# Infini-attention with a gated feed-forward on one core: memory reads and their scaling moved into the gate/up phases, value projections moved between the first transposes, phi in two VectorE steps

## Chip, core and metric

The kernel runs on one core of one Trainium2 chip. The metric is device time of one execution in microseconds (us). Before the change the median of 14 runs is 299.04 us (296.95 to 301.62).

## What is computed

The input x has 2048 rows of 448 columns in bfloat16, H = 16 heads of Dh = 28 columns, and the rows are cut into 4 segments of L = 512. The reference, cut to what matters:

```python
xn = layernorm(x)
q, k, v = xn @ wq, xn @ wk, xn @ wv          # (B, H, segment, L, Dh)
phi = lambda t: where(t > 0, t + 1.0, exp(t))
g = sigmoid(beta)
M = 0; z = 0
for s in range(4):
    p = softmax(q[s] @ k[s].T * Dh ** -0.5 + causal_mask)
    a_dot = p @ v[s]
    a_mem = (phi(q[s]) @ M) / (phi(q[s]) @ z + 1e-6)
    out[s] = g * a_mem + (1 - g) * a_dot
    M += phi(k[s]).T @ v[s]; z += phi(k[s]).sum(rows)
S = concat(out) @ wo
G = silu((gelu(xn @ w_gate) * (xn @ w_up)) @ w_down)   # w_gate, w_up: 448 x 1792
return x + S * G
```

## The kernel before

The order of the work is written out by hand (`tc.manual_schedule()`): every engine runs its instructions in the order in which the program issues them, and TensorE, VectorE, ScalarE and GpSimd each wait at their own head of queue. All DMAs on SP likewise stand in one queue. So "later in the program" means "behind" on every engine that an operation uses.

**Tiles.** A segment has NB = 4 blocks of 128 rows; D = 448 is padded to NDC = 4 chunks of 128; heads go in G = 4 groups of HG = 4, each head padded to 32 columns. Queries and keys are kept transposed (head columns on partitions, 512 rows along the free axis), values with rows on partitions and a column of ones beside each head (`vaug`), so that a product with V also gives the softmax's sum. PSUM has three pools: `ps_s` (two tiles of 128 x 1024, for scores and for gate/up), `ps_pv` (one), `ps_m` (three tiles named `m`, for all else).

**Stages** (times of the profiled execution):

- Head, 0 to 29.3 us: 100 idle matmuls on zeros (line 93), loads, layer norm of segment 0 (`layer_norm`, lines 226 to 263), per block a scaling on VectorE (`scale_x`, line 250), four TensorE transposes and a ScalarE copy (`turn`, lines 260 and 261), then `project_units(0)`: eight q/k units (line 302) and four v units (line 335, evicted on VectorE at line 337). One pair of tiles `xns` holds the scaled blocks in turn.
- Gate/up 0, 29.3 to 57.4 us: `gate_up` (line 466 on) has 14 steps `fc`. Each has four matmuls with w_gate and four with w_up into one `s` tile (line 474), a gelu on ScalarE (`gl`, line 477), a product on VectorE (`hT`, line 478), and whatever a table of steps holds for step `fc`. At full clock a step is 1.73 us of TensorE. In steps of gate/up 0 stand the layer norm of segment 1 (transposed by DMA, line 256) and `guard`, a check of the weights' size whose squares go into tiles named `pqT` and `xr`.
- Attention 0, 57.4 to 90; gate/up 1, 90 to 113.8; attention 1, 113.8 to 157.9; gate/up 2 and 3, 157.9 to 207; attention 2, 207 to 234; attention 3, 234 to 268.
- Tail, 268 us to the end: the rest of segment 3's down projections (`d3[2:]`, 18 units), its last combinations and the output.

**Attention** (`attention`). There are 12 score steps k (4 groups x 3 banks). Step k issues scores on TensorE (line 378), exp on ScalarE (line 384), a causal mask on GpSimd (line 388), and the product with V of step k-2 (line 399, `give`). Each step has two half steps; in each, a table `at` may add work, and filler units (projections of the next segment, down projections, output products) are issued while the TensorE work done is less than `due`, which the planner computes: `own` and `ours` are its costs of scores and products in us, `tot` the cost of all filler, `theirs` the running ScalarE cost (1.3, 1.3 or 0.88 per half step; 27.84 at the end).

```python
theirs.append((theirs or [0.0])[-1] + (1.3, 1.3, 0.88)[bk])
...
due = (own + tot) * theirs[n - 1] / theirs[-1] - ours[n - 1]
```

The last two products of a segment are returned as `ends` and issued in the stage after.

**phi** (lines 312 to 328) follows a projection by two ticks of a clock: exp on ScalarE (line 315); then, a tick later, three VectorE steps: u = t + 1 (line 319), e = min(e, 1) (line 321), max(u, e) (line 323). phi(k) goes into a tile `pkT` of a pool with two buffers, and SP transposes it by DMA into `pkb` (line 325). phi(q) goes into `pqT`.

**Dividing.** `evac` (line 407 on) copies an accumulated product to SBUF (VectorE, line 412) and sends the rows with the sums by SP to a compact tile `dc` (line 416). `invert` (line 425 on) scales and inverts `dc` on VectorE (lines 430 and 432), splits it on GpSimd into three bf16 `terms` (lines 435 and 437) and sends them by SP into `rows` (line 438). `inverses` (line 446) spreads `rows` over the partitions by a matmul into an `m` tile. `combine` (lines 458, 462, 463) scales the attention part with it and adds the memory part; `scale_memory` (line 451) scales the memory part; `memory_read` (line 422) multiplies phi(q) with the memory and calls `evac`.

**Where these stand before.** The memory reads of segments 1 and 3 are the first filler of attentions 1 and 3 (`pre`), their inversion and scaling stand in the table `at`. Those of segment 2 stand in gate/up 3. The last two products, the inversion and the combinations of segment s are issued by `tail`, in the next gate/up phase (segment 2: in attention 3; segment 3: in the tail).

## Time and profile before

| What | Value |
|---|---|
| Median of 14 runs | 299.04 us (296.95 to 301.62) |
| The profiled execution's own time | 300.53 us |
| Its span, first to last instruction | 298.7 us |
| Mean granted TensorE clock | 0.956 |
| Mean of one gelu (line 477), ScalarE | 597 ns |
| Mean of one exp, 1024 and 512 columns (line 384) | 1021 ns and 598 ns |
| Mean of one table load, ScalarE | 1283 ns |
| Mean of one copy of 512 columns out of PSUM, VectorE (line 412) | 681 to 686 ns |
| phi's three steps, VectorE (lines 319, 321, 323) | about 300, 530, 450 ns |

The profile is of one execution. PE is TensorE's matmul, PEld its weight loads, DVE VectorE, ACT ScalarE, POOL GpSimd, SP the engine that issues most DMAs; a q behind the name is the engine's sequencer. "L474" is line 474 of the kernel. "out<-in" names the tiles. In brackets or after the bar stands the idle time of the engine just before, and the instruction that ended it. The row PEclk gives in 40 slices the clock that TensorE was granted, in tenths of full speed. Matmuls overlap, so a busy share near 1 for TensorE does not say that the array works at its peak.

### The profile page before, as it was taken

The page shows a single profiled execution, that of the slowest core. Times are in us where ns is not written, and L with a number is a line of the kernel's source. Part 1 is how long each engine was busy: PE and PEld are TensorE (multiplying, and loading weights), DVE is VectorE, ACT ScalarE, POOL GpSimd, SP SyncE. Part 2 cuts the span into 40 slices and gives each one's busy share as a digit, 9 for nine tenths or more (in the row PEclk, how much of TensorE's full clock was granted, in tenths as well). Part 3 has the DMA queues.
Part 4 walks back from the last instruction along what each step waited for, and adds up shares of the span by engine and source line. Part 5 has one row for each costly group of instructions (what it writes and reads, how often), then busy time and mean ns, then how long its engine had stood idle before and what let it go on. Part 6 is the DMA issues. An engine that isn't in the chain of part 4 may idle for free. (4 is left out here: it accounts for less than half of the span.)

```text
span 298.7 us, 4626 instructions
## 1 busy us (share of the span) xinstructions
PE 264.2 (88%) x1652; PEld 116.6 (39%) x1652; DVE 189.3 (63%) x381; ACT 151.3 (51%) x215; POOL 98.0 (33%) x217
## 2 busy tenths in 40 slices
PE   7695999989999997989999999999799879893960
PEld 7442344434444443333344444544233323341420
DVE  6655376346687767478787666557566634862863
ACT  3352264569894333786673333334979566760010
POOL 4100010044440300765450233120667455485000
PEclk9887799999999999999999999999899968999798
DMA  8998002300100053001110120001000000001002
GB/s 242 357 329 111 18 2 50 82 2 1 38 19 19 9 98 101 3 24 34 35 35 19 26 53 2 4 8 61 15 19 16 24 7 10 3 32 36 3 5 69
DMA packets 26354, 15.11 MB, mean 51 GB/s; under 512 B 17872, under 2 KB 25044, under 8 KB 26324
## 3 DMA queue, kind: packets, MB, share of 16 engines
q1 hardware_dynamic: 23392, 10.20, 14.7%
q10 hardware_dynamic: 2324, 3.16, 3.2%
q0 software_dynamic: 608, 1.38, 1.3%
q8 instruction: 15, 0.25, 0.3%
q14 instruction: 15, 0.12, 0.1%
HBM read 9.18 MB, written 1.84 MB: 37 GB/s over the span
## 5 line engine op out<-in xcount | busy, mean ns | idle before, releaser
L384 ACT ACTIVATE pt<-s 128x1024 bf16<-128x1024 f32 (+1 forms) x96 | 79.1, 880 | 24.5 <-PE s L378 22.8
L388 POOL TENSOR_SCALAR_AFFINE_SELECT pt<-pt 128x256 bf16<-128x256 bf16 x128 | 50.5, 417 | 86.7 <-ACT pt L384 85.0
L477 ACT ACTIVATE gl<-s 128x512 bf16<-128x512 f32 x56 | 33.4, 597 | 70.6 <-PE s L474 51.7
L478 DVE TENSOR_TENSOR hT<-gl,s 128x512 bf16<-128x512 bf16 x56 | 38.4, 686 | 36.4 <-ACT gl L477 35.6
L474 PE MATMUL s<-xnT,wg_sb 128*128 128x512 bf16 x224 | 58.9, 386 | 0.2 <-DVE hT L478 0.2
L474 PE MATMUL s<-xnT,wu_sb 128*128 128x512 bf16 x224 | 58.4, 384 | 0.0
L489 PE MATMUL m<-wd_sb,hT 128*128 128x448 bf16 x224 | 52.9, 369 | 0.9 <-DVE oU L462 0.9
L474 PEld LDWEIGHTS <-wu_sb 128*128 128x128 bf16 x224 | 22.1, 99 | 27.1 <-issue 1.1
L474 PEld LDWEIGHTS <-wg_sb 128*128 128x128 bf16 x224 | 21.9, 100 | 27.3 <-issue 3.1
L489 PEld LDWEIGHTS <-hT 128*128 128x128 bf16 x224 | 21.4, 101 | 24.8 <-issue 7.3
L378 PE MATMUL s<-qT,kT 32*128 32x512 bf16 (+3 forms) x256 | 21.8, 312 | 5.8 <-ACT pt L384 5.6
L246 POOL TENSOR_TENSOR rstd<-rstd,nhalf 128x2 f32<-128x2 f32 x8 | 5.7, 707 | 57.1 <-DVE rstd L244 57.1
L302 PE MATMUL m<-xnT,wq_pad 128*128 128x512 bf16 x64 | 17.8, 395 | 2.2 <-ACT xnT L261 0.9
L492 ACT ACTIVATE th<-m 128x448 f32<-128x448 f32 x16 | 8.6, 546 | 21.4 <-PE m L489 16.3
L335 PE MATMUL m<-wv_sb,xnT 128*128 128x448 bf16 x64 | 15.9, 381 | 3.8 <-DVE vaug L337 3.5
L399 PE MATMUL pv<-pt,vaug 128*32 128x512 bf16 (+3 forms) x256 | 18.2, 317 | 1.0 <-POOL pt L388 0.6
L378 PEld LDWEIGHTS <-kT 32*128 32x128 bf16 x256 | 6.8, 92 | 27.2 <-issue 26.9
L302 PE MATMUL m<-xnT,wk_pad 128*128 128x512 bf16 x64 | 17.4, 391 | 0.0
L306 DVE CAST kT<-m 128x512 bf16<-128x512 f32 x16 | 11.0, 686 | 9.6 <-PE m L302 9.5
L412 DVE COPY oU<-pv 128x512 f32<-128x512 f32 x16 | 11.0, 686 | 9.5 <-PE pv L399 9.4
L446 PE MATMUL m<-rows,spread 128*128 128x512 bf16 x28 | 11.1, 402 | 6.4 <-DMA rows<-terms 6.1
L518 PE MATMUL m<-wo_sb,oT 128*128 128x448 bf16 x64 | 15.2, 360 | 0.9 <-DVE oT L463 0.9
(100 smaller groups left out, 282.5 us busy)
## 6 DMA issues: line engine op xcount, KB each, us to landing
x_sb<-in_A_x_dram SPq DMA_DIRECT2D x7, 224.0 KB
wd_sb<-in_B_w_down_dram SPq DMA_DIRECT2D x1, 1568.0 KB
wg_sb<-in_B_w_gate_dram SPq DMA_DIRECT2D x1, 1344.0 KB
wu_sb<-in_B_w_up_dram ACTq DMA_DIRECT2D x1, 1344.0 KB
out_dram<-o_out POOLq DMA_DIRECT2D x12, 112.0 KB, 2.0
xr<-in_A_x_dram ACTq DMA_DIRECT2D x2, 448.0 KB
out_dram<-o_out SPq DMA_DIRECT2D x4, 112.0 KB
wo_sb<-in_A_wo_dram SPq DMA_DIRECT2D x4, 98.0 KB
```

The costliest lines, as they stand in the source:

```text
L302: nc.tensor.matmul(out=pr[:], lhsT=wpad[nm][:, c, g * HG:(g + 1) * HG, :].rearrange("p h d -> p (h d)"), rhs=xnT[s][:, c, :], start=(c == ...
L335: nc.tensor.matmul(out=vp[:, 0:D], lhsT=xnT[s][:, c, b * P:(b + 1) * P], rhs=wv_sb[:, c, :], start=(c == 0), stop=(c == NDC - 1))
L378: nc.tensor.matmul(out=sp[i // 2][:, i % 2, c0:c0 + n], lhsT=kT[s][r, g, kb * P:(kb + 1) * P], rhs=qT[s][r, g, kb * P:L], start=True, stop ...
L384: nc.scalar.activation(out=pt[:, :, 0:w], in_=sp[pr][:, :, 0:w], func=ACT.Exp, scale=scale)
L388: nc.gpsimd.affine_select(out=v, in_=v, pattern=[[0, 2], [1, P]], compare_op=ALU.is_ge, fill=0.0, base=0, channel_multiplier=-1)
L399: nc.tensor.matmul(out=acc[i * HP:(i + 1) * HP, kb * P:L], lhsT=va[:, kb, g * HG + i, :], rhs=pts[i // 2][:, i % 2, c0:c0 + n], start=(kb ...
L446: nc.tensor.matmul(out=r[:], lhsT=spread[:, g, :], rhs=rows[side][:], start=True, stop=True)
L474: nc.tensor.matmul(out=gu[:, i, :], lhsT=w_sb[:, c, fc * P:(fc + 1) * P], rhs=xnT[s][:, c, :], start=(c == 0), stop=(c == NDC - 1))
L477: nc.scalar.activation(out=gl[:], in_=gu[:, 0, :], func=ACT.Gelu_apprx_tanh)
L478: nc.vector.tensor_tensor(out=hT[s][:, fc, :], in0=gl[:], in1=gu[:, 1, :], op=ALU.mult)
L489: nc.tensor.matmul(out=d_ps[:, 0:D], lhsT=hT[s][:, fc, b * P:(b + 1) * P], rhs=wd_sb[:, fc, :], start=(fc == 0), stop=(fc == NFC - 1))
L518: nc.tensor.matmul(out=a_ps[:, 0:D], lhsT=oT[s][:, g, b * P:(b + 1) * P], rhs=wo_sb[:, g, :], start=(g == 0), stop=(g == G - 1))
```

## The change

The diff touches six things.

1. The head issues 145 idle matmuls, and issues the v unit of block b-1 after block b's transposes; the last v unit follows the padding of wk. The eight q/k units come after.
2. phi takes two VectorE steps: e = min(e, 1), then one `scalar_tensor_tensor` that computes max(t + 1, e). The pool of `pkT` has three buffers; for segment 0, phi(k) has a tile of four slots, which takes the buffer named `pqT`.
3. `theirs` in attention begins from 2.6 instead of 0.
4. `evac` can copy on ScalarE. It does for the last product of segments 0 and 1 and for the memory reads of segments 1 and 2, all in gate/up phases.
5. Memory reads, inversion and scaling of segment 1 go from attention 1 into gate/up 1 (steps 0 to 3, 6, 10 to 13), where the inversion of segment 0's sums goes from step 5 to 4 and its combinations from steps 10 on to 7 on. In gate/up 3 the inversion goes from step 6 to 4, the scaling from 10 to 8. The reads of segment 3 go from the start of attention 3 to half steps 5 to 8, their inversion to 13, their scaling to 17 to 20; there segment 2's inversion goes from half step 5 to 4 and its combinations from 10 to 9.
6. In the tail the first inversion splits its terms on VectorE, and the three combinations begin one unit later, so that the last group's inversion stands ahead of the third of them.

```diff
-        pkp = pool("pkp", 2)
+        pkp = pool("pkp", 3)
...
-        for i in range(100):
+        for i in range(145):
...
+            units0.extend(project_units(0))
+            v = units0[8:]
             for b in range(NB):
                 scale_x(b)
                 turn(b)
+                if b:
+                    run(v[b - 1:b])
             pad_weight("wk")
+            run(v[NB - 1:])
...
+            if s == 0:
+
+                pk0 = seg1.tile([P, G, L], BF16, name="pqT")
+
             def phi(g, nm, dst):
                 e = work.tile([P, L], BF16, name="ph_e")
-                u = seg1.tile([P, L], BF16, name="ph_u")
                 nc.scalar.activation(out=e[:], in_=dst[:, g, :], func=ACT.Exp)
-                ph = pqT[s][:, g, :] if nm == "wq" else pkp.tile([P, L], BF16, name="pkT")[:]
+                if nm == "wq":
+                    ph = pqT[s][:, g, :]
+                else:
+                    ph = pk0[:, g, :] if s == 0 else pkp.tile([P, L], BF16, name="pkT")[:]
 
                 def rest():
-                    nc.vector.tensor_scalar(out=u[:], in0=dst[:, g, :], scalar1=1.0, scalar2=None,
-                                            op0=ALU.add)
                     nc.vector.tensor_scalar(out=e[:], in0=e[:], scalar1=1.0, scalar2=None,
                                             op0=ALU.min)
-                    nc.vector.tensor_tensor(out=ph, in0=u[:], in1=e[:], op=ALU.max)
+                    nc.vector.scalar_tensor_tensor(out=ph, in0=dst[:, g, :], scalar=1.0, in1=e[:],
+                                                   op0=ALU.add, op1=ALU.max)
...
-            nc.vector.tensor_copy(out=t, in_=ps[:])
+            (copy or nc.vector.tensor_copy)(out=t, in_=ps[:])
...
-                    theirs.append((theirs or [0.0])[-1] + (1.3, 1.3, 0.88)[bk])
+                    theirs.append((theirs or [2.6])[-1] + (1.3, 1.3, 0.88)[bk])
...
+        units0 = []
         layer_norm_first()
-        run(project_units(0))
+        run(units0[:8])
...
-        table = tail(0, {}, ends, 5, 10)
+        table = tail(0, {}, ends, 4, 7, nc.scalar.copy)
+        memory(1, table, 0, 6, 10, nc.scalar.copy)
...
-        pre = [(0.22, [lambda g=g: memory_read(1, g)]) for g in range(G)]
-        at = memory(1, {}, 99, 5, 10, 2)
-        ends = attention(1, pre + merge([(0.9, [lambda: update(1)])], pu[8:12])
-                         + merge(down_units(1), finish_units(0), pu[:8]), at)
+        ends = attention(1, merge([(0.9, [lambda: update(1)])], pu[8:12])
+                         + merge(down_units(1), finish_units(0), pu[:8]))
...
-        table = tail(1, {}, ends, 5, 10)
+        table = tail(1, {}, ends, 5, 10, nc.scalar.copy)
...
-        table = memory(2, {}, 0, 6, 10)
+        table = memory(2, {}, 0, 4, 8, nc.scalar.copy)
...
-        at = tail(2, {}, ends, 5, 10)
-        pre = [(0.22, [lambda g=g: memory_read(3, g)]) for g in range(G)]
-        memory(3, at, 99, 6, 14, 2)
-        ends = attention(3, pre + d2[2:] + merge(finish_units(2), d3[:2]), at)
+        at = memory(3, tail(2, {}, ends, 4, 9), 5, 13, 17)
+        ends = attention(3, d2[2:] + merge(finish_units(2), d3[:2]), at)
...
-        table = {0: [lambda: invert(3, 0, 0, G - 1)], 1: ends[:1], 3: ends[1:],
+        table = {0: [lambda: invert(3, 0, 0, G - 1, nc.vector)], 1: ends[:1], 3: ends[1:],
                  8: [lambda: invert(3, 0, G - 1, G, **fast)]}
-        in_turn(table, 5, [lambda g=g: combine(3, g) for g in range(G - 1)])
+        in_turn(table, 6, [lambda g=g: combine(3, g) for g in range(G - 1)])
```

## The prediction

> **What bounds the kernel now.** I read busy shares first, then busy time by stage, then TensorE's waits, then the timeline around each long wait. The page:

> ```profile
> PE 264.2 (88%) x1652; PEld 116.6 (39%) x1652; DVE 189.3 (63%) x381; ACT 151.3 (51%) x215; POOL 98.0 (33%) x217
> ...
> PEclk9887799999999999999999999999899968999798
> ```

> TensorE is the bound on average, but its clock row dips in four regions: the first 35 us, and around 215, 245 and 278 us. Cutting the span at the stage borders shows where it is not full (time, PE busy, PEld, DVE, ACT, POOL, clock):

> ```profile
> 0.00:29.30 29.30, 21.61 (x165) 14.01 (x165) 17.27 (x56) 11.07 (x16) 4.99 (x13) 0.90 0.96 265
> ...
> 157.90:207.00 49.10, 49.07 (x240) 22.75 (x240) 31.57 (x58) 15.75 (x27) 11.06 (x18) 1.00 0.07 15
> 207.00:234.00 27.00, 24.39 (x185) 9.00 (x184) 18.23 (x33) 23.01 (x29) 17.55 (x38) 0.94 0.11 35
> 234.00:268.00 34.00, 30.01 (x219) 11.35 (x217) 19.13 (x33) 21.65 (x28) 18.48 (x48) 0.90 0.05 13
> 268.00:298.70 30.70, 15.53 (x78) 6.65 (x76) 16.50 (x30) 2.06 (x4) 5.78 (x12) 0.91 0.09 28
> ```

> Gate/up of segments 2 and 3 (157.9 to 207) is solid TensorE; nothing off TensorE can be gained there. Head, attention 2, attention 3 and tail have holes. TensorE's waits, in total, times, longest:

> ```profile
> PE m L446 <- DMA rows<-terms: 6.1, 2, 4.5
> PE s L378 <- ACT pt L384: 5.6, 9, 1.2
> PE m L335 <- DVE vaug L337: 3.5, 2, 3.4
> ...
> PE m L422 <- DVE oT L458: 1.4, 1, 1.4
> ```

> The clock by 3.4 us stretches gives the second half of the price. Stretches with PE busy 1.10 (23.4:26.8), 1.41 (9.8:13.2), 1.90 (211.2:214.6), 1.75 (238.5:241.9) and 0 us (272.6:276) were each followed by half clock; stretches at 2.28 (112.2:115.6), 2.31 (269.2:272.6) and 2.43 us (231.7:235.1) were not. So holes cost twice.

> ```profile
> 211.20:214.60 3.40, 1.90 (x22) 0.70 (x21) 1.86 (x3) 2.81 (x5) 3.09 (x7) 1.00 0.09 34
> 214.60:218.00 3.40, 3.40 (x26) 0.98 (x18) 1.72 (x5) 2.55 (x4) 1.38 (x4) 0.50 0.02 5
> ```

> [...]

> **The change, part by part.** Times are of the profiled execution (300.53 us, span 298.7).

> *Head.* Now the third phi result waits 3.48 us for one of two pkT buffers, held by a DMA transpose; the v evictions queue behind it on VectorE, TensorE waits 3.35 us, and the clock is halved until 33.7. Gate/up 0 starts at 29.30 with 4.4 us of half clock ahead, worth 2.2 us: as if at 31.5. In the new order segment 0's phi(k) gets four slots (no wait), and v runs among the transposes. The 45 extra idle matmuls at some 0.055 us (the rate of the last 55 of the 100: 3.0 us) end near 11.9, so block 0's transposes slip from 11.22 by 0.7 us. Then a serial chain: copy of block 0 (589 ns), v 0 (4 matmuls, 0.75), its eviction 0.62, and only behind it on VectorE the scaling of block 2 (0.38); transposes 0.25, v 1, and so on, about 2.2 us per block with handoffs. v 3 ends near 19.1, then eight q/k units of 0.86: gate/up starts near 26. The order of ScalarE shows a cost that the diff hides: the fourth phi(k) now falls behind the first gelu, so exp and gelu tables are loaded again: 2 x 1.283 + 0.63 = 3.2 us between the first two gelus. Gelu 1 ends 6.2 us after the stage starts, the VectorE product at 6.9, while TensorE wants that buffer for its fourth step at 5.2: 1.7 us of stall. Behind these loads on ScalarE wait all later gelus; the check's squares must also wait for the phi buffer, which carries the same name, about 0.3 us and covered. Effective start 27.7 against 31.5: 3.8 us gained with a full clock. The chain keeps TensorE busy about 2.0 us per 3.4, between 1.90 (halved) and 2.28 (kept), so I cannot decide it; half clock costs 1.5 to 3. I take 2.5, range 0.5 to 4.

> *phi in two steps.* Three rows, 310 + 530 + 442 ns, become 530 + x; x lies between 442 (as the two-tensor row) and about 690 (612 scaled by 512/448). I take 690: 0.06 us x 24 = 1.5 us of VectorE; at 442, 7 us. The cover is TensorE; nothing is counted apart.

> *Earlier fill in attention (the 2.6).* Filler matmuls are due sooner, by 2.6/30.44 = 8.5% of a stage's TensorE work at its start, none at its end. Attention 0: scores wait 0.63 us for exp at 63.3 and v 0.34 us earlier; 0.7 taken (0 to 1). Attention 2: waits 1.07 and 0.63 us plus the half clock of 214.6:218, which costs about 1.5; but ScalarE has 24.9 us of work there (16 x 1.021 + 8 x 0.598 = 21.1, four phi exps 2.5, a table load 1.3) in 27.0, so at most 2.1 to 2.5. Taken 1.5 (0 to 2.5).

> *Memory reads of segment 1.* At 114 to 117 us four reads wait for VectorE: excesses of 1.5, 0.4 and 0.4 us, 2.3 in all. They go into gate/up 1, evicted by ScalarE (about 0.6 us each; it has 1.13 us idle per step there). Matmuls, 8 x 0.22 with the scalings, move and do not vanish. VectorE in attention 1 loses 4 x 0.68 + 4 x 0.68 = 5.4 us, and TensorE waits 0.57, 0.50, 0.28 and 0.23 us behind VectorE in it; some of that goes, and with the earlier fill the 0.58 us at 121.3. Taken 2.8 (1.5 to 4). In gate/up 1 the first inversion now has three steps (5.2 us) until its rows are read; in the trace of before this takes 4.65 us from VectorE's step (100.65) to landing (third DMA issued at 103.25 plus 2.0, as in the tail). VectorE at up to 2.05 us in one step of 1.73 is covered by two score buffers. The new dc and rows DMAs pass SP ahead of the x transposes, delaying block 1's by about 2 us; the last still lands before attention 1. Taken -0.2 (-1 to 0). Gate/up 3: the inversion comes two steps earlier and VectorE waits about 0.4 us for dc, covered.

> *Attention 3.* Four reads leave its start: 0.78 + 0.57 + 0.22 us wait, while ScalarE idles 3.58. Then scores wait 1.19 and 0.63, and two half-clock stretches (241.9 to 248.7) of 5.9 us of matmul time lose 3.0. At 254 one more 0.95 us wait, for PSUM. Sum 7.3; what is late next is ScalarE, 24 exps and four tanh in 34. The reads come back at half steps 5 to 8, evicted by VectorE. I take half: 3.5 (1 to 6).

> *Tail.* The longest wait:

> ```profile
> 271.87 0.56 POOL L530 DMA_DIRECT2D out_dram<-o_out  x1 [0.30 <-POOL o_out L529]
> 272.43 0.25 POOL L435 CAST terms<-dc 96x64 bf16<-96x64 f32 x1
> 272.70 2.66 SPq L438 DMA_DIRECT2D rows<-terms  x3
> ...
> 275.46 0.59 SPq L416 DMA_DIRECT2D dc<-oU  x1
> ...
> 276.63 0.59 PE L446 MATMUL m<-rows,spread 128*128 128x512 bf16 x1 [4.47 <-DMA rows<-terms]
> ```

> The reciprocal was ready at 269.6; GpSimd, behind masks and outputs, took it up at 272.43. On VectorE the five small operations (0.19 to 0.22) end at 270.8, three issues on SP of 0.8 end near 272.5, rows landed near 273.5: 3.1 us earlier. The combine moves one unit (0.58 us) later, so 4.5 us of wait become about 0.8; with that hole the half clock of 276:279.4 (about 1.4) likely goes. The last group's dc DMA, behind these on SP, issues near 272.5 instead of 275.46, and its inversion now stands ahead of the third combine (1.37 us). Left at the end, about 1 us instead of 1.68. Sum 5.7; the output chain after it (12 us) is unchanged. I take 4.2 (1.5 to 5.7).

> **Sum.** 2.5 + 0.7 + 1.5 + 2.8 - 0.2 + 3.5 + 4.2 = 15.0: 285.5 from the profiled 300.53. That execution is 1.5 above the median of 299.04; some of the 1.5 may be clock loss already in the sum. I put 285.

> **Rivals.**
> *The clock is not granted.* Holes shrink but stay thin, head and both late attentions stay half clocked, or ScalarE binds: head 1.0, attention 0 0.7, gate/up 1 -0.2, attention 1 2.8, attention 2 0.3, attention 3 1.5, tail 3.5: 9.6, so 291. For: the head's 2.0 lies in the undecided gap. Against: the tail's wait is a plain queue on GpSimd.
> *Everything goes.* Upper ends, about 22: 278. For: the terms are separate waits. Against: ScalarE's 24.9 us in attention 2.
> *Slower: fill starves ScalarE.* In-order TensorE puts 8.5% of a stage's 28 to 40 us (2.4, 3, 1.8, 1.8 = 9.0 us) ahead of the scores; if ScalarE is then the bound to each stage's end, it is lost in full and replaces the 8.5 us that attentions gain: 300.5 - 2.5 + 0.2 - 4.2 + 9.0 = 303. It decides once more than about 6.5 of the 9.0 us is lost. For: ScalarE waits 22.8 us for scores in all. Against: in attentions 0 and 1 it has slack (30.18 of 44.1 busy in attention 1).

> **How the numbers follow.** About 0.3% is what a measurement can tell from no change. Forecast (281 to 288) 0.58; clock not granted (288 to 296) 0.23; everything 0.14; slower 0.04; no change 0.01. The range 279.5 to 291.5 leaves out the far ends.

> **What would show it.** Right: no wait of TensorE on v's eviction, full clock after about 20 us, two more table loads of 1283 ns after the first gelu with one stall of 1 to 2 us, reads without waits in gate/up 1, terms on VectorE in the tail with its row wait under 1.5 us. Wrong: half clock from 16 to 24 us, a row wait in gate/up 1 over 1 us, attention 3 still near 34 us, or phi's second step well over 0.7 us.

## The result and the profile after

The changed kernel takes 294.92 us (median of 10 runs, 293.91 to 297.93), the kernel before 299.28 (median of 47 runs): a ratio of 0.989 with a 95% interval of 0.986 to 0.992. The ratios count the fast runs of a kernel alone, those within 1.5% of the fastest beside them, and by that rule the profiled executions of the kernel before and of experiment 7 are slow ones. The changed kernel is faster, by 4.4 us instead of the 14 that I forecast, and lies outside my range. Its profiled execution took 294.19 us with a span of 292.2, against 300.53 and 298.7 before, so 6.5 us of the span are to be explained. About 2 of them come from the choice of the two executions, since one lies 0.7 us below its kernel's median and the other 1.3 above. Differences below between two variants are of medians; where they are small the ratios to the kernel before decide, since each was taken with runs of that kernel on the same chip.

The page of the kernel after, busy time by engine and TensorE's granted clock in 40 slices:

```profile
PE 260.1 (89%) x1697; PEld 116.9 (40%) x1697; DVE 185.1 (63%) x352; ACT 157.7 (54%) x227; POOL 100.3 (34%) x212
...
PEclk9999999999999999999999999999999999796698
```

The dips of the first 35 us and of 215 us are gone. What is left sits in the last fifth, and there it is deeper than before. The same by stage (time, busy of PE, PEld, DVE, ACT, POOL, clock, then DMA share and GB/s): head, gate/up 0 with attention 0, gate/up 1 with attention 1, gate/up 2 and 3, attention 2, attention 3, tail.

```profile
0.00:25.90 25.90, 21.80 (x209) 15.76 (x210) 16.07 (x48) 8.86 (x14) 4.99 (x13) 1.00 0.94 286
25.90:84.40 58.50, 56.25 (x357) 24.21 (x356) 36.86 (x72) 42.01 (x60) 16.84 (x36) 1.00 0.16 33
84.40:145.10 60.70, 60.27 (x391) 26.24 (x389) 44.70 (x81) 38.89 (x57) 24.85 (x52) 1.00 0.18 42
145.10:199.20 54.10, 53.91 (x271) 24.57 (x269) 32.85 (x60) 21.64 (x37) 12.38 (x21) 1.00 0.08 17
199.20:225.80 26.60, 24.62 (x189) 9.26 (x188) 17.32 (x28) 22.82 (x29) 18.49 (x40) 1.00 0.12 37
225.80:258.60 32.80, 27.45 (x211) 10.31 (x210) 19.55 (x34) 21.33 (x28) 19.40 (x46) 0.95 0.05 13
258.60:292.20 33.60, 15.81 (x77) 6.53 (x76) 17.70 (x34) 2.17 (x4) 3.32 (x6) 0.81 0.08 25
```

Five stages run at a full clock; only the last two do not. Reading where stages start in the two timelines (the first gate/up matmul, the first and the last score) gives the balance in us. (These borders replace the stage times given ahead of the forecast, which lie up to 4.5 us later: gate/up 2 starts at 153.4, not at 157.9.)

| stretch | before | after | change | my step |
|---|---|---|---|---|
| head and gate/up 0 | 0 to 59.0 | 0 to 55.4 | -3.6 | -2.5 |
| attention 0 | 59.0 to 88.1 | 55.4 to 84.4 | -0.1 | -0.7 |
| gate/up 1 and attention 1 | 88.1 to 153.4 | 84.4 to 145.1 | -4.6 | -2.6 |
| gate/up 2 and 3 | 153.4 to 207.6 | 145.1 to 199.2 | -0.1 | 0 |
| attention 2 and 3, to the last score | 207.6 to 265.7 | 199.2 to 256.2 | -1.1 | -5.0 |
| tail, from the last score | 265.7 to 298.7 | 256.2 to 292.2 | **+3.0** | -4.2 |

The row of attention 2 and 3 hangs on the execution. Experiment 3 below runs the program of the kernel before, changed in the tail alone, and in its profiled execution every other stretch ahead of the tail agrees with this table within 0.2 us. Attention 2 and 3, however, take 55.4 us there (207.8 to 263.2) instead of 58.1. The two, from 27.7 us after the first score of attention 2 on, first the kernel before, then experiment 3:

```profile
235.30:265.70 30.40, 26.98 (x201) 9.98 (x199) 17.43 (x30) 20.56 (x26) 15.53 (x39) 0.89 0.05 10
235.50:263.20 27.70, 24.32 (x200) 9.75 (x200) 17.54 (x30) 20.45 (x26) 15.45 (x39) 1.00 0.05 11
```

The same instructions run once with a stretch of half clock and once without it, 2.7 us apart. Against experiment 3 the changed kernel's 57.0 us are 1.6 us slower, not 1.1 faster.

At 199 us the kernel is 8.4 us ahead, more than the 5.8 that my steps give to that point. The tail gives 3.0 back where I had 4.2 to gain. TensorE's waits (total, times, longest) name the cause:

```profile
PE m L456 <- DMA rows<-terms: 10.8, 4, 5.9
PE s L388 <- ACT pt L394: 3.4, 10, 0.6
PE s L484 <- DVE hT L488: 2.2, 3, 1.8
```

The v evictions are no longer among the long waits (3.5 us before), and the scores wait 3.4 us instead of 5.6. But the spread matmuls wait 10.8 us for inverse rows, where it was 6.1. The longest of these waits, in the timeline of the tail: VectorE's first cast of the terms, two row waits of TensorE, and the DMA issues of SP and GpSimd.

```profile
259.12 1.68 DVE L445 CAST terms<-dc 96x64 bf16<-96x64 f32 x1
260.86 2.66 SPq L448 DMA_DIRECT2D rows<-terms  x3
264.78 0.38 PE L456 MATMUL m<-rows,spread 128*128 128x512 bf16 x1 [2.60 <-DMA rows<-terms]
...
269.68 0.68 SPq L448 DMA_DIRECT2D rows<-terms  x1
...
271.31 0.64 POOL L448 DMA_DIRECT2D rows<-terms  x1 [9.72 <-issue]
273.12 0.61 PE L456 MATMUL m<-rows,spread 128*128 128x512 bf16 x1 [5.91 <-DMA rows<-terms]
```

Three groups' rows were sent from 260.86 and the first combines used them at 264.78 and 265.37. The third combine needs no other row. Yet its spread matmul at 273.12 waits 5.91 us, until just behind the row DMAs of 269.68 to 271.31, which carry the rows of the last group, for which it has no use. In the code the reason is in two lines: `combine(3, 2)` now falls on unit 8, behind the last group's inversion of the same unit, and the spread matmul takes all of `rows[side]` as its operand (L456), into which that inversion writes (L448 to L449). The clock is half from 265.85 to 276.09, three windows of 3.41 us. The first stands behind the wait of 2.60 us and begins before the hole of 5.91 us; the hole keeps the clock down for two more. (From 262.44 on TensorE is busy 0.97, 1.28, 0 and 2.97 us of each 3.41; the last three of these are at half clock.)

In attention 3 the same pair of operations waits again. The timeline, then a cut in stretches of 3.4 us:

```profile
244.95 1.92 SPq L448 DMA_DIRECT2D rows<-terms  x3
248.25 0.38 PE L456 MATMUL m<-rows,spread 128*128 128x512 bf16 x1 [2.04 <-DMA rows<-terms]
```

```profile
236.00:239.40 3.40, 2.50 (x16) 0.84 (x17) 3.08 (x5) 3.17 (x5) 2.27 (x5) 1.00 0.11 21
239.40:242.80 3.40, 3.02 (x25) 1.14 (x25) 3.33 (x6) 1.78 (x3) 0.95 (x3) 1.00 0.00 1
...
246.20:249.60 3.40, 1.36 (x12) 0.43 (x8) 1.20 (x2) 0.77 (x2) 3.09 (x7) 0.88 0.11 17
249.60:253.00 3.40, 3.15 (x18) 0.87 (x15) 1.25 (x2) 1.94 (x2) 1.58 (x4) 0.62 0.10 34
```

The memory inversion of segment 3 starts at half step 13 (243.64 on VectorE), and its rows arrive after the scaling wants them; TensorE then has 1.36 us of work in 3.4 and loses the clock. VectorE is full from 236 to 242.8 (3.08 and 3.33 us), which made me suspect the four reads that now stand there.

### The profile page after: what moved, and what is told of

The parts are those of the page before. It is cut to its first block, busy times and chain, and to the rows that moved or that the text cites. A ratio compares the mean times of both kernels' runs of the same rounds, so it can differ in the third digit from the quotient of the medians.

```text
span 292.2 us, 4695 instructions
## 1 busy us (share of the span) xinstructions
PE 260.1 (89%) x1697; PEld 116.9 (40%) x1697; DVE 185.1 (63%) x352; ACT 157.7 (54%) x227; POOL 100.3 (34%) x212
## 3 DMA queue, kind: packets, MB, share of 16 engines
q0 software_dynamic: 608, 1.38, 1.3%
## 5 line engine op out<-in xcount | busy, mean ns | idle before, releaser
L398 POOL TENSOR_SCALAR_AFFINE_SELECT pt<-pt 128x256 bf16<-128x256 bf16 x128 | 53.8, 444 | 80.4 <-ACT pt L394 79.4
L484 PE MATMUL s<-xnT,wg_sb 128*128 128x512 bf16 x224 | 57.5, 379 | 2.2 <-DVE hT L488 2.2
L484 PE MATMUL s<-xnT,wu_sb 128*128 128x512 bf16 x224 | 57.5, 379 | 0.0
L499 PE MATMUL m<-wd_sb,hT 128*128 128x448 bf16 x224 | 52.0, 364 | 0.2 <-DVE oU L472 0.2
L499 PEld LDWEIGHTS <-hT 128*128 128x128 bf16 x224 | 20.8, 100 | 23.3 <-issue 6.4
L456 PE MATMUL m<-rows,spread 128*128 128x512 bf16 x28 | 11.1, 401 | 12.1 <-DMA rows<-terms 10.8
L409 PE MATMUL pv<-pt,vaug 128*32 128x512 bf16 (+3 forms) x256 | 17.5, 311 | 0.0
L307 PE MATMUL m<-xnT,wq_pad 128*128 128x512 bf16 x64 | 17.0, 380 | 0.0
L422 DVE COPY oU<-pv 128x512 f32<-128x512 f32 x14 | 9.6, 683 | 10.4 <-PE pv L409 10.4
L311 DVE CAST qT<-m 128x512 bf16<-128x512 f32 x12 | 8.3, 690 | 11.1 <-PE m L307 11.0
L345 PE MATMUL m<-wv_sb,xnT 128*128 128x448 bf16 x64 | 14.7, 353 | 0.6 <-ACT xnT L261 0.5
```

The costliest lines, as they stand in the source:

```text
L307: nc.tensor.matmul(out=pr[:], lhsT=wpad[nm][:, c, g * HG:(g + 1) * HG, :].rearrange("p h d -> p (h d)"), rhs=xnT[s][:, c, :], start=(c == ...
L345: nc.tensor.matmul(out=vp[:, 0:D], lhsT=xnT[s][:, c, b * P:(b + 1) * P], rhs=wv_sb[:, c, :], start=(c == 0), stop=(c == NDC - 1))
L398: nc.gpsimd.affine_select(out=v, in_=v, pattern=[[0, 2], [1, P]], compare_op=ALU.is_ge, fill=0.0, base=0, channel_multiplier=-1)
L409: nc.tensor.matmul(out=acc[i * HP:(i + 1) * HP, kb * P:L], lhsT=va[:, kb, g * HG + i, :], rhs=pts[i // 2][:, i % 2, c0:c0 + n], start=(kb ...
L456: nc.tensor.matmul(out=r[:], lhsT=spread[:, g, :], rhs=rows[side][:], start=True, stop=True)
L484: nc.tensor.matmul(out=gu[:, i, :], lhsT=w_sb[:, c, fc * P:(fc + 1) * P], rhs=xnT[s][:, c, :], start=(c == 0), stop=(c == NDC - 1))
```

## The experiments

My theory after the result: the mechanisms in head, attention 1 and attention 2 were right; two edges of the new order cost what the rest of the change gains, the false dependency in the tail and the late inversion in attention 3. Rivals: the late inversion's place on VectorE and SP costs, whichever tile it writes; the reads crowd VectorE; the earlier fill does harm.

**1. The last group's inversion one unit later**, behind the third combine.

```diff
-                 8: [lambda: invert(3, 0, G - 1, G, **fast)]}
+                 9: [lambda: invert(3, 0, G - 1, G, **fast)]}
```

> The changed kernel with the last group's inversion in the tail issued after the third combination (unit 9, not 8); TensorE's order is the same. Theory: the third combination's spread matmul reads the whole rows tile, so in the changed kernel it waits for the last group's rows DMAs, which the program issues just ahead of it; that is the 5.91 us wait at 273.1 us and the reason for half clock until 276. Then the wait falls under 0.5 us, and although the inversion itself comes 1.4 us later on VectorE the time falls by about 5 us, to about 290. Rival: the last group's rows set the end anyway (its inversion is on the path, and it is now later): no gain, or up to 1 us slower, 295 to 296.

Measured: 288.09 us (287.78 to 291.15), ratio 0.964 (0.960 to 0.969). One digit gives 6.8 us. Third and last spread matmul of its tail:

```profile
267.44 0.58 PE L456 MATMUL m<-rows,spread 128*128 128x512 bf16 x1 [0.27 <-DVE oU L472]
274.62 0.39 PE L456 MATMUL m<-rows,spread 128*128 128x512 bf16 x1 [0.93 <-DMA rows<-terms]
```

The 5.91 us are gone from the third; the last group's own wait is 0.93 us. Behind the first row wait (2.63 us here) one window is at half clock, 266.38 to 269.79, instead of three, and another from 276.62 (the 13 output matmuls from 276.52 take 4.32 us, 2.63 in experiment 2). So the place matters. It doesn't yet tell the tile from the queues.

**2. A row buffer of its own for the last group**, with the order left as it is after the change: its inverses are written into `rows[1]` and read from there.

```diff
-                    out=rows[side][32 * i + g0 * HG:32 * i + g1 * HG, :].rearrange(
+                    out=rows[side if to is None else to][32 * i + g0 * HG:32 * i + g1 * HG, :].rearrange(
...
-            o_a, r, dst = oU.pop((s, g, 0)), inverses(0, g), oT[s][:, g, :]
+            o_a, r, dst = oU.pop((s, g, 0)), inverses(int(s == NSEG - 1 and g == G - 1), g), oT[s][:, g, :]
...
-        fast = dict(eng=nc.vector, queues=[nc.sync, nc.scalar, nc.gpsimd])
+        fast = dict(to=1, eng=nc.vector, queues=[nc.sync, nc.scalar, nc.gpsimd])
```

> The kernel after with its order unchanged; only the last group's inverses are written into and read from the other row buffer, so that the combine of the third group no longer depends on the last group's row transfers. Theory (the dependency on a shared tile is what costs): the 5.91 us wait goes and the time falls as in the run with unit 9, to 288 to 290. Rival (the queue places of the late inversion cost, on VectorE and SP, whichever tile it writes): no change, 294 to 296.

Measured: 287.32 us (286.92 to 289.52), ratio 0.959 (0.954 to 0.963). Its third and last spread matmul:

```profile
269.89 0.38 PE L456 MATMUL m<-rows,spread 128*128 128x512 bf16 x1 [0.59 <-DVE oU L472]
275.75 0.39 PE L456 MATMUL m<-rows,spread 128*128 128x512 bf16 x1 [0.76 <-DMA rows<-terms]
```

The inversion still stands ahead of the third combine on VectorE and SP, and the wait is gone all the same. It was the shared tile, not the queues. From the last score (259.0) to the end of the span (287.7) it takes 28.7 us, 4.3 less than before: the tail's gain that I had forecast (4.2). The same tail in the second combination of experiment 10 takes 29.6 us (252.1 to 281.7), with one window of half clock at 261.45 that this execution lacks: the third spread matmul takes 0.59 us there and 0.38 here.

**3. The terms of the tail on VectorE alone, in the kernel before.**

```diff
-        table = {0: [lambda: invert(3, 0, 0, G - 1)], 1: ends[:1], 3: ends[1:],
+        table = {0: [lambda: invert(3, 0, 0, G - 1, nc.vector)], 1: ends[:1], 3: ends[1:],
```

> The kernel before with one edit: the terms of the first inversion of the tail are computed on VectorE instead of GpSimd; the combines stay at units 5 to 7, ahead of the last group's inversion at unit 8. Theory (my tail step was right about the terms and failed only on the order of the third combine): the first row wait falls from 4.47 us to about 2.5 and part of the half clock behind it goes, 1.5 to 4 us less than before, 295.5 to 298. Rival (the terms were never what the rows waited for, SP's queue was): no change, 298.5 to 300.

Measured: 297.54 us (296.53 to 299.05), ratio 0.993 (0.990 to 0.996). Its VectorE and SP at the start of the tail, and its first row wait:

```profile
267.90 1.29 DVE L435 CAST terms<-dc 96x64 bf16<-96x64 f32 x1
269.22 0.22 DVE L437 TENSOR_TENSOR dc<-dc,terms 96x64 f32<-96x64 f32 x1
```

```profile
272.16 0.57 PE L446 MATMUL m<-rows,spread 128*128 128x512 bf16 x1 [2.44 <-DMA rows<-terms]
```

The wait of 4.47 us falls to 2.44, not to 0.8. The part alone gains 2.2 us (0.7% of 299.9; 1.3 to 3.0 by the interval). The two traces don't place it: of their 3.3 us of span 0.8 lies in the tail (32.2 us from the last score instead of 33.0), and 2.7 in attention 3, where the programs are the same.

**4. The memory inversion of segment 3 at half step 11 instead of 13.**

```diff
-        at = memory(3, tail(2, {}, ends, 4, 9), 5, 13, 17)
+        at = memory(3, tail(2, {}, ends, 4, 9), 5, 11, 17)
```

> The changed kernel with the inversion of segment 3's memory sums in attention 3 at half step 11 instead of 13 (its rows are read from half step 17). Theory: attention 3 lost its gain to a new wait, the rows landing 2.0 us too late for the first scaling at 248.3 us, and the half clock that this hole brings (248.8 to 252.2): 2 to 3.5 us faster, 291.5 to 293. Rival: attention 3 is bound by ScalarE, and the wait only takes up slack: within 0.5 us of 294.9.

Measured: 293.23 us (292.72 to 293.56), ratio 0.980 (0.977 to 0.983). Its row wait, and the stretch behind it:

```profile
247.05 0.38 PE L456 MATMUL m<-rows,spread 128*128 128x512 bf16 x1 [0.81 <-DMA rows<-terms]
```

```profile
248.80:252.20 3.40, 2.60 (x22) 0.96 (x21) 2.06 (x4) 1.86 (x3) 2.56 (x6) 1.00 0.10 34
```

2.04 us of wait became 0.81, and the half clock of attention 3 went. By medians this is 1.7 us, a little under the theory's range. Attention 2 and 3 take 54.8 us from the first score of attention 2 (199.1) to the last of attention 3 (253.9), against 57.0 after the change.

**5. Attention 3 arranged as before**: reads first as filler, output units from 5 and 10, inversion at 6, scalings at 14, 16, 18, 20.

```diff
-        at = memory(3, tail(2, {}, ends, 4, 9), 5, 13, 17)
-        ends = attention(3, d2[2:] + merge(finish_units(2), d3[:2]), at)
+        at = tail(2, {}, ends, 5, 10)
+        pre = [(0.22, [lambda g=g: memory_read(3, g)]) for g in range(G)]
+        for i, f in enumerate([lambda: invert(3, 1)]):
+            at.setdefault(6, []).append(f)
+        for i in range(G):
+            at.setdefault(14 + 2 * i, []).append(lambda g=i: scale_memory(3, g))
+        ends = attention(3, pre + d2[2:] + merge(finish_units(2), d3[:2]), at)
```

> Attention 3 alone is arranged as in the kernel before: the four memory reads of segment 3 as filler at its start, output units from half steps 5 and 10, memory inversion at 6, scalings at 14, 16, 18, 20; all else as in the kernel after (294.9 us). Theory: the rearrangement of attention 3 cost about as much as it gave, since the reads at half steps 5 to 8 fall on a VectorE that is full (3.08 and 3.33 of 3.40 us) and the late inversion makes TensorE wait 2.04 us for rows: 293.5 to 296.0. Rival (my prediction's step, 3.5 us gained by moving the reads): undoing it costs 2 us or more, 297 to 299.

Measured: 291.83 us (291.25 to 292.5), ratio 0.974 (0.970 to 0.979). Better than my theory had it, and far from the rival's 297 to 299: undoing this part gains about 3 us. Attention 2 and 3 take 54.5 us (198.5 to 253.0), at a full clock.

**6. The reads alone put back**, with the inversion at 11.

```diff
-        at = memory(3, tail(2, {}, ends, 4, 9), 5, 13, 17)
-        ends = attention(3, d2[2:] + merge(finish_units(2), d3[:2]), at)
+        at = tail(2, {}, ends, 4, 9)
+        in_turn(at, 11, [lambda: invert(3, 1)])
+        in_turn(at, 17, [lambda g=g: scale_memory(3, g) for g in range(G)])
+        pre = [(0.22, [lambda g=g: memory_read(3, g)]) for g in range(G)]
+        ends = attention(3, pre + d2[2:] + merge(finish_units(2), d3[:2]), at)
```

> The kernel after with the four memory reads of segment 3 as filler at the start of attention 3, as before, and the inversion at half step 11; the rest of attention 3 stays as in the kernel after (output units from 4 and 9, scalings from 17). It differs from the run with half step 11 (293.23) only in where the reads stand. Theory (the reads at half steps 5 to 8 crowd VectorE and cost by themselves): 290.5 to 292.3, as with the whole arrangement of before (291.83). Rival (only the late inversion cost anything, the place of the reads is neutral): 292.8 to 294.

Measured: 293.09 us (291.84 to 294.49), ratio 0.978 (0.975 to 0.982), the same as with the reads at 5 to 8 (0.980). My theory of a crowded VectorE falls:

```profile
236.00:239.40 3.40, 2.93 (x21) 1.04 (x21) 2.52 (x4) 3.32 (x5) 2.11 (x6) 1.00 0.03 8
```

VectorE has 2.52 us of work here instead of 3.08 and TensorE 2.93 instead of 2.50, but the reads wait for it elsewhere, 0.57 and 0.22 us at 224.6 and 225.2. Where the reads stand is neutral here, with the earlier fill in place; the late inversion cost. Whether an inversion at 6 is better than one at 11 (0.974 against 0.978) the intervals leave open.

**7. No earlier fill** (the 2.6 set to 0).

```diff
-(theirs or [2.6])
+(theirs or [0.0])
```

> The changed kernel with the planner's offset 2.6 set back to 0 (filler as before). Theory: the early fill gave about half of what attentions 1 and 2 gained (4.6 and 2.4 us): 2 to 4 us slower, 297 to 299. Rival A: it gave nothing (the reads' move did it all): within 0.5 us. Rival B: it starves ScalarE: 1 us or more faster.

Measured: 298.63 us (295.16 to 301.23), ratio 0.996 (0.993 to 0.998). The intervals of the ratios just lie apart (0.992 and 0.993). By the medians of all runs the fill is worth 3.7 us, by those that the ratio counts 3.4 (298.28). It is the opposite of my slower rival, in which it starved ScalarE. Its profiled execution was above its median (300.17), so I take from it only the places: the scores of attention 1 last 31.2 us (114.2 to 145.4) against 29.0, and the clock is halved again in attention 2 and 3 (0.50 from 207.5 to 210.9 and from 234.8 to 241.6).

**8. The deferred evictions emitted ahead of the ninth gate/up unit**, so that the fourth phi's exponential stands before the first gelu.

```diff
         run(units0[:8])
+        flush()
```

> The changed kernel with the pending phi steps of segment 0 issued before gate/up 0 begins, so that the fourth exp of phi(k) stands before the first gelu. Theory: the two added table loads and the 1.80 us wait of TensorE for the product in gate/up 0 go: 1.8 us faster, 293.1. Rival: the exp put ahead of the first gelu delays it, or the wait was slack given back later: within 0.5 us of 294.9.

Measured: 293.23 us (292.42 to 295.05), ratio 0.979 (0.976 to 0.982). ScalarE after the change, from its first gelu on:

```profile
27.86 0.60 ACT L487 ACTIVATE gl<-s 128x512 bf16<-128x512 f32 x1 [0.17 <-PE s L484]
28.48 1.28 ACT L323 ACT_TABLE_LOAD   x1
29.77 0.63 ACT L323 ACTIVATE ph_e<-kT 128x512 bf16<-128x512 bf16 x1
30.42 1.28 ACT L487 ACT_TABLE_LOAD   x1
```

and with the one line added:

```profile
28.82 0.63 ACT L323 ACTIVATE ph_e<-kT 128x512 bf16<-128x512 bf16 x1 [0.47 <-DVE kT L311]
29.47 1.28 ACT L487 ACT_TABLE_LOAD   x1
30.76 0.60 ACT L487 ACTIVATE gl<-s 128x512 bf16<-128x512 f32 x1
```

Two table loads are gone, and TensorE's wait for the product falls from 2.2 to 1.0 us in all.

**9. 100 idle matmuls at the start instead of 145.**

```diff
-range(145)
+range(100)
```

> The kernel after with 100 idle matmuls at the start instead of 145; nothing else. [...] Theory (the head's chain of transposes and v projections lies at the edge of what keeps the clock[...]): either 293.5 to 295.5 with a full clock and the first transposes up to 0.7 us earlier, or 296 to 298 with one half-clock stretch between 12 and 24 us. Rival (the added matmuls are what keeps the head at full clock): half clock from 12 us on for two stretches, over 297.

Measured: 298.45 us (296.73 to 300.14), ratio 0.995 (0.993 to 0.997). The rival holds, with three windows at half clock (11.67 to 21.91). TensorE's first transposes, and the windows from 8.26 us:

```profile
11.23 0.82 PE L260 MATMUL m<-ident,xn 128*128 128x128 bf16 x8 [2.35 <-DVE xn L250]
```

```profile
8.26:11.67 3.41, 1.06 (x19) 0.81 (x17) 3.05 (x11) 0.69 (x2) 1.43 (x2) 1.00 1.03 393
11.67:15.08 3.41, 2.13 (x9) 0.63 (x8) 0.93 (x2) 1.07 (x2) 0.06 (x1) 0.50 1.04 298
15.08:18.50 3.42, 2.40 (x12) 1.15 (x13) 0.93 (x2) 0.59 (x1) 0.00 (x0) 0.50 1.06 315
18.50:21.91 3.41, 3.41 (x12) 1.39 (x10) 1.30 (x3) 0.59 (x1) 0.00 (x0) 0.50 1.10 334
```

Without the added 45 the hole ahead of the transposes halves the clock, and the serial chain behind it is too thin to win it back for 10 us: gate/up starts at 28.6 instead of 25.9. I had priced these matmuls only at what they cost (0.7 us). They bring most of what head and gate/up 0 gain together: the first score of attention 0 stands at 59.0 before, at 58.1 here and at 55.4 after the change, so 2.7 of 3.6 us.

**10. Repairs together.** Later inversion in the tail (1), inversion at 11 (4) and flush (8):

> The kernel after with the last group's inversion at unit 9 instead of 8, the memory inversion of segment 3 at half step 11 instead of 13, and the deferred evictions emitted before the ninth gate/up unit. Theory: the three act at different places, so their gains (6.8, 1.7 and 1.7 us) add: 284 to 286.5. Rival: the gains overlap through the clock (a stretch saved in one place turns cold in another): 287 to 289.

Measured: 284.87 us (284.33 to 286.44), ratio 0.952 (0.947 to 0.957). The gains add: 6.8 + 1.7 + 1.7 = 10.2 from 294.9 is 284.7. Own buffer (2), attention 3 as before (5) and flush (8):

> The kernel after with attention 3 arranged as before, an own row buffer for the last group's inverses, and the deferred evictions emitted before the ninth gate/up unit. Theory (three separate places, gains of 3.1, 7.6 and 1.7 us add): 281 to 284. Rival (the own buffer's gain contains part of the others through the clock): 284.5 to 287.

Measured: **283.54 us** (282.04 to 285.06), ratio 0.945 (0.941 to 0.949), the fastest of the study, 5.5% under the kernel before and 1 us above the plain sum (282.5). And a more eager tail, beside (2), (4) and (8):

```diff
-                 8: [lambda: invert(3, 0, G - 1, G, **fast)]}
-        in_turn(table, 6, [lambda g=g: combine(3, g) for g in range(G - 1)])
+                 6: [lambda: invert(3, 0, G - 1, G, **fast)]}
+        in_turn(table, 9, [lambda g=g: combine(3, g) for g in range(G - 1)])
```

> As the last one (own row buffer for the last group), with the last group's inversion moved up to unit 6 and the three combines to units 9, 10 and 11, the memory inversion at half step 11, and the deferred evictions emitted before the ninth gate/up unit. Theory: the first row wait (2.60 us) is covered by three more units of 0.58 us and the last group's rows land before the units end: 282 to 285. Rival: with the combines later the last combine becomes the end of a chain that the units no longer cover, and nothing is gained over the plain sum: 285 to 288.

Measured: 286.96 us (286.39 to 288.42), ratio 0.959 (0.954 to 0.963), worse than the plain repairs and outside the theory's range: the last score starts at 252.7 as in the first of these (252.6), so the 1.8 us of span are lost in the tail, where the second combine now waits for VectorE.

```profile
PE m L456 <- DVE wg_sb L506: 3.9, 1, 3.9
```

## Why the prediction was wrong, step by step

- **Tail: the step that failed.** I wrote that the combine "moves one unit (0.58 us) later, so 4.5 us of wait become about 0.8" and that the last group's inversion "now stands ahead of the third combine (1.37 us)". I saw the new order and priced it as VectorE's busy time. Its price was the last group's reciprocal, terms and row DMAs, because that inversion writes the tile which the third combine's matmul reads: a wait of 5.91 us and two more windows of half clock. The tail missed its forecast by 7.2 us; experiments 1 and 2 gain 6.8 and 7.6. With only the dependency removed, the tail gains 4.3 us, and 3.4 in the second combination (forecast 4.2).
- **Tail, sizes.** First row wait 2.60 us instead of 0.8. From the reciprocal's end (259.03) to the last term's (261.76) VectorE took 2.7 us, not 1.2, for its first cast took 1.68 us where the next two of the same shape took 0.19. It ends within 0.1 us of GpSimd's output add: the cast at 260.80, the add at 260.73. In experiment 3 the cast of 1.29 us ends at 269.19, the add (268.11, 1.03 us) at 269.14. Each cast was recorded ahead of the add, from 259.12 (the add from 259.70) and from 267.90, while a mask ran on GpSimd. No run removes the add, so that the cast waited for GpSimd is a reading of this coincidence and not shown. GpSimd in the kernel after:

```profile
258.97 0.77 POOL L398 TENSOR_SCALAR_AFFINE_SELECT pt<-pt 128x256 bf16<-128x256 bf16 x2
259.70 1.03 POOL L539 TENSOR_TENSOR o_out<-sg,x_sb 128x448 bf16<-128x448 f32 x1
```

- **Attention 2 and 3: -1.1 instead of -5.0.** Three things failed in these steps. The half clock of attention 3, 3.0 of the 7.3 us of which I took half, belonged to the execution and not to the order: experiment 3 ran the same instructions without it. The waits at the start of attention 3 I put down to the place of the reads, and experiment 6 shows moving them to be worth nothing once the fill is earlier. And the late inversion, which I priced in gate/up 1 but not in attention 3, cost 2.2 us in the traces (experiment 4). Without it the two attentions gain 2.7 to 3.6 us on the profile before (experiments 4 to 6), but only 0 to 0.9 on that of experiment 3. I put what is gained down to the earlier fill; experiment 7 points that way but doesn't separate the stages.
- **Head: the size right, at its upper end; one term mis-sized.** Gate/up 0 starts at 25.94 (I had "near 26"), the stall behind the table loads is 1.80 us (1.7). The clock, which I could not decide, stayed full in this execution, and experiment 9 shows that the 45 idle matmuls, for me only a cost of 0.7 us, are what kept it: 2.7 of the 3.6 us.
- **Attention 1: right, too small.** 4.6 with gate/up 1 instead of 2.6; about 2 of it is the fill by the places of experiment 7. The rest I put down to the reads; no run moves these alone. **Attention 0**: 0.1 instead of 0.7.
- **phi.** 0.69 us for the second step, as I took it. I had scaled it from the one such operation in the kernel before (`sg<-th,m`, line 496, 612 ns at 448 columns), which has a float PSUM operand: 1.37 ns per column. With bf16 on all sides the row below takes 1.35 ns per column, against 0.86 for the two-tensor row (442 ns at 512).

```profile
23.61 0.69 DVE L332 SCALAR_TENSOR_TENSOR pqT<-kT,ph_e 128x512 bf16<-128x512 bf16 x1
```

- **Rivals.** "The clock is not granted" came nearest in time (291), for other reasons; the starved ScalarE is refuted by experiment 7. (In that rival's sum 2.4, 3, 1.8 and 1.8 us are 8.5% of some 28, 35, 21 and 21 us, not of the 28 to 40 written beside them.)

With the own buffer, attention 3 as before and the flush the change gives 283.5 us, near the 285 that I forecast, but the nearness is in part luck. On the profile before, head and gate/up 0 gain 5.3 us (forecast 2.5), gate/up 1 and attention 1 4.7 (2.6), attention 2 and 3 3.6 (5.0) and the tail 3.4 (4.2).

## What to carry to other kernels

When a step moves past another in a table, ask of each pair which tile both touch and with what extent, not only which engine: here a matmul that reads a whole tile waited 5.91 us for DMAs issued earlier into a part of it that it had no use for. Price a moved producer by its whole chain to the reader (here reciprocal, terms, DMA), in every stage in which it moves. And price fill or idle work at what it keeps alive, the clock, as well as at its own time (here 2.7 us against 0.7). A stretch of half clock is a gain to be had only if it comes back in another execution of the same program.

## What the runs showed of the hardware

I worked out an array share for each window: columns streamed, at 512 per 216 ns at full clock (the pitch of matmuls in gate/up after the change, whose recorded times of 379 ns overlap) and twice that at half (in gate/up 0 before the pitch was 427 ns at 31 us), weighted by the share of rows and columns that a tile uses, and counted from each matmul's recorded start. Of the 158 windows of the two profiles between 5 and 280 us, the seven at full clock with a share of 0.34 or less were followed by half clock, and the 141 at full clock with 0.42 or more by full clock. From half clock six windows with a share of 0.86 or more came back, and four with 0.76 or less did not. But the same columns take twice the share at half clock, so this is nearly one edge in columns. If each matmul's columns are spread evenly over its recorded time, one edge fits all 158 windows at either clock: up to 3038 columns of the whole array were followed by half clock, 3399 and more by full clock, where a full window at full clock holds 8091 (3.413 us at 512 per 216 ns). The share is an estimate of mine from the matmul records of these two profiles, not a counter.

**The head is a toss.** With 145 idle matmuls the chain of transposes lies at the edge: the window of 14.05 to 17.45 us held 1.51 and 1.46 us of TensorE work in experiments 8 and 2, whose profiled executions were halved behind it. In the kernel after and in the second combination of experiment 10 the clock read 1.00 up to 25.9 and 25.5 us. The code up to the first q and k units is the same in all four. In the kernel after the stretch of 14.05 to 17.45 us holds no more work (1.42 us), but there the grid falls at 13.26 and 16.68 us, and the poorest window of the chain holds 1.88 us.

```profile
14.05:17.45 3.40, 1.46 (x10) 0.53 (x8) 1.80 (x4) 0.58 (x1) 0.00 (x0) 1.00 1.06 350
17.45:20.85 3.40, 3.29 (x12) 1.62 (x13) 1.20 (x3) 0.58 (x1) 0.00 (x0) 0.50 1.09 315
```

These are the two windows of experiment 2's head. The two of the kernel after:

```profile
13.26:16.68 3.42, 1.88 (x12) 0.73 (x10) 1.40 (x3) 0.81 (x2) 0.00 (x0) 1.00 1.05 360
16.68:20.09 3.41, 2.90 (x17) 1.43 (x18) 2.14 (x5) 0.59 (x1) 0.00 (x0) 1.00 1.08 306
```
